# RWKV attention, FFN and top-1 MoE chained on one core: the first three attention tiles re-queued over VectorE and GpSimd, and the raw-weight transposes moved behind the third product

## The chip, the cores and the metric

The kernel runs on one core of one Trainium2 chip. The metric is device time of one launch in microseconds (us), and a kernel's time is the median of its runs.

## What is computed

Three stages follow one another, each on 3072 tokens (4 batches of 768) of 384 features (8 heads of 48), in fp32 with fp64 inputs for the weights of the last two:

```python
# 1. attention, per batch and head
for t in range(S):
    cur = einsum('bhd,bhe->bhde', u * k[t], v[t])
    y[t] = einsum('bhd,bhde->bhe', r[t], state + cur)
    state = w * state + einsum('bhd,bhe->bhde', k[t], v[t])
# 2. FFN, 384 -> 2048 -> 384
h = x @ w_in
g = h - tanh(h)
x = g @ w_out
# 3. top-1 mixture, 8 experts of 384 -> 1024 -> 384
xn, en = x / |x|, emb / |emb|
logits = xn @ en.T / tau
out = gate * (relu(x @ w1[e]) @ w2[e])   # e = argmax(logits)
```

## The kernel before

**Attention** works on 24 tiles of 128 tokens, three to a block of 384 tokens. With the decay tables `tab_r` and `tab_k` (powers of w along the tile, built by `decay_tables`, lines 194 to 208) a tile is a few matrix products. `Att` holds its steps: `products` multiplies r by k (L376), `decay_r` and `decay_k` scale r and k by the tables (L355, L358), `summed` sums the products per head with u (TensorE L382, copied by ScalarE L384), `diagonal` writes those sums on a diagonal (ScalarE L405, eight instructions, tile `am`), `scores` multiplies keys by queries (L423, PSUM tiles `pa`), `causal` copies the lower triangle of the scores over `am` (VectorE L428, two instructions), `values` multiplies by the values (L454, PSUM tile `py`), and `result_hi` and `result_lo` write the result as a rounded part and the rest (ScalarE L459, VectorE L462). `turned` and `turned_rows` transpose the scaled keys (L364) and copy them out (ScalarE L369, `ktok`); `state_product` (L475) and `state_add` carry the state on.

**The FFN** goes over its 2048 hidden features in steps of 128. `ffn1` computes one step for a block: nine matmuls of 128x384 (L557), since activations and weights are both split in a rounded and a rest part. `squares` and `small_tanh` turn its result into h - tanh(h) (from ScalarE L612 on), and `ffn2` multiplies that by w_out into three accumulators (L572). The weights come as fp64 chunks; `convert` turns the bits into fp32 on VectorE (L264, L267, L270, each in two pieces), and `split` makes the two parts on ScalarE (L277) and GpSimd (L278). The first chunk is converted and split in two halves, the others whole. The odd chunks hold w_out; `Logits.turn` transposes such a raw chunk (six TensorE transposes L293, two copies L295) for products with the expert embeddings (L303).

**PSUM** has eight banks, handed out in the order in which the program asks. A filler is a matmul on a tile of ones whose result is overwritten (`fill`, L547): `scores`, `values` and `ffn1` take their number as `idle`, and the table `IDLE` gives it for the first six steps of the main loop.

**Order.** Each engine works through its queue in program order, and the opening (lines 1310 to 1386) is written out by hand: the steps of tiles `a[0]` to `a[2]`, the first chunk's conversion, and the expert embeddings' norms (`embedding_norms` ScalarE L1243, `embedding_roots` VectorE L1246 and a GpSimd power L1247, `embedding_rows` VectorE L1250 to L1252). Then the first two products of the first block (`early`) are issued, and the loop over `steps` (L1442 on) issues one product for each step, with a piece of the following tiles (`attention_stage`: the fourth to sixth tile), a chunk's conversion and, where due, `Logits.turn`, `done` and `load_next`, which starts the next chunk's load. The third product is that of step 2, the fourth that of step 3. The first accumulation of `ffn2` stands behind the fifth product, and from there on the products and accumulations of the FFN follow one another.

## Time and profile before

| what | value |
|---|---|
| median of 3 runs | 769.78 us |
| lowest and highest run | 769.21 us, 770.74 us |
| profiled execution, its own time | 771.22 us |
| its span, first to last instruction | 769.6 us |
| mean granted clock of TensorE in it | 0.995 |
| TensorE busy | 756.2 us, 98% of the span |

The profiled execution lies 1.44 us above the median, and 1.6 us of its time lie outside the span. Times inside it are microseconds from the start of the span. TensorE's work is busy time as the profiler's records model it, so a busy share says that something was in the array, not that it ran at full clock; the granted clock is a column of its own.

### The profile page before, as it was taken

The numbers are of one execution on the slowest core, as the hardware profiler recorded it, in microseconds if no ns is written. First come the engines' busy times: TensorE is split into PE (matmuls) and PEld (weight loads), VectorE is DVE, ScalarE is ACT, GpSimd is POOL, SyncE is SP. The second block draws the span as 40 slices with busy tenths as digits, with TensorE's granted clock in tenths as the row PEclk, the third lists the DMA queues.
The fourth block names the chain that finished last, engine by engine and source line by source line (L and its number), as shares of the span: only waits on it lengthen the run. The fifth ranks groups of instructions, "written<-read, shape, count | busy, mean of one in ns | idle before, by whom it ended". The sixth has DMA issues, their size and how long they took to land.

```text
span 769.6 us, 15995 instructions
## 1 busy us (share of the span) xinstructions
PE 756.2 (98%) x6143; PEld 718.4 (93%) x6143; DVE 464.8 (60%) x1037; ACT 457.1 (59%) x1064; POOL 300.5 (39%) x362
## 2 busy tenths in 40 slices
PE   9899999999999999999999999999999999999996
PEld 5689899999999999999999999999989999999996
DVE  7967976667656565565555655656684455545430
ACT  5787676655657556656657756768463535544431
POOL 3743680466781671753564341133530202110111
PEclk9899999999999999999999999999999999999999
DMA  8964355243240330232223101052374435454400
GB/s 263 288 206 142 118 170 200 64 165 100 66 148 24 126 122 2 91 94 87 80 69 123 59 32 64 14 171 85 116 229 143 129 115 189 150 173 161 154 31 32
DMA packets 41016, 92.21 MB, mean 120 GB/s; under 512 B 4827, under 2 KB 20597, under 8 KB 39907
## 3 DMA queue, kind: packets, MB, share of 16 engines
q1 hardware_dynamic: 36274, 81.44, 33.0%
q0 software_dynamic: 4240, 9.67, 3.5%
q8 instruction: 50, 0.82, 0.4%
q14 instruction: 36, 0.29, 0.1%
q10 hardware_dynamic: 416, 0.00, 0.0%
HBM read 67.26 MB, written 24.00 MB: 119 GB/s over the span
## 4 chain that ended last, share of the span: by engine, by line
PE 90%; issue 3%; DVE 3%; ACT 2%; DMA 2%; POOL 1%; POOLq 0%; SPq 0%; DVEq 0%; ACTq 0%
PE acc L572 39%; PE ph L557 37%; PE py L454 5%; PE pa L423 3%; DMA eraw<-in_moe_w_dram 2%; PE pt L908 1%; PE warm L158 1%; PE pst L475 1%; POOL out_dram L827 0%; PE pt L293 0%; DVE bits L267 0%; DVE wraw L270 0%; PE pl L303 0%; DVE bits L264 0%; PE accn L1036 0%
## 5 line engine op out<-in xcount | busy, mean ns | idle before, releaser
L557 PE MATMUL ph<-xt,wq 128*128 128x384 f32 (+4 forms) x1712 | 340.1, 341 | 1.9 <-ACT wt L295 1.3
L557 PEld LDWEIGHTS ph<-xt,wq 128*128 128x128 f32 x1712 | 302.7, 188 | 5.9 <-ACT wt L295 1.5
L572 PE MATMUL acc<-wq,ghi 128*128 128x392 f32 (+2 forms) x1120 | 289.1, 343 | 0.9 <-ACT ghi L625 0.9
L572 PEld LDWEIGHTS acc<-wq,ghi 128*128 128x128 f32 (+1 forms) x1120 | 200.3, 187 | 5.9 <-ACT ghi L625 1.2
L572 PE MATMUL acc<-wq,glo 128*128 128x392 f32 (+2 forms) x552 | 182.2, 340 | 0.1
L612 ACT ACTIVATE z<-ph 128x384 f32<-128x384 f32 x128 | 62.8, 490 | 105.0 <-PE ph L557 104.7
L623 DVE TENSOR_TENSOR ph<-ph,z 128x384 f32<-128x384 f32 x128 | 72.0, 563 | 62.6 <-ACT z L612 62.0
L572 PEld LDWEIGHTS acc<-wq,glo 128*128 128x128 f32 (+1 forms) x552 | 102.7, 187 | 0.9 <-DVE glo L635 0.7
L635 DVE TENSOR_TENSOR glo<-ph,ghi 128x384 fp32r<-128x384 f32 x128 | 70.7, 553 | 45.7 <-ACT ghi L625 45.6
L827 POOL DMA_INDIRECT out_dram<-ob,gts x27 | 27.2, 1008 | 176.6 <-ACT ob L917 171.4
L625 ACT ACTIVATE ghi<-ph 128x384 fp32r<-128x384 f32 x128 | 62.6, 490 | 41.0 <-DVE ph L624 37.6
L615 ACT ACTIVATE q<-z,sb_t 128x384 f32<-128x384 f32 x128 | 78.9, 617 | 3.4
L624 DVE SCALAR_TENSOR_TENSOR ph<-q,ph 128x384 f32<-128x384 f32 x128 | 71.7, 560 | 12.5 <-ACT q L615 3.5
L629 ACT ACTIVATE mk<-z,lz_t 128x384 bf16<-128x384 f32 x128 | 77.1, 603 | 0.0
L653 DVE SCALAR_TENSOR_TENSOR glo<-ph,ghi 128x384 fp32r<-128x384 f32 (+2 forms) x56 | 30.7, 549 | 63.8 <-ACT ghi L651 63.8
L651 ACT ACTIVATE ghi<-ph 128x384 fp32r<-128x384 f32 (+4 forms) x56 | 27.5, 491 | 67.6 <-PE ph L557 67.5
L411 POOL TENSOR_TENSOR am<-ident,cd 128x512 f32<-128x512 f32 x36 | 36.8, 1045 | 77.8 <-DVE cd L397 77.1
L886 DVE TENSOR_TENSOR wq<-eraw,wq 128x768 fp32r<-128x768 f32 x60 | 55.1, 955 | 11.5 <-ACT wq L885 11.0
L885 ACT ACTIVATE wq<-eraw 128x768 fp32r<-128x768 f32 x64 | 50.4, 839 | 6.2 <-DMA eraw<-in_moe_w_dram 6.2
L278 POOL TENSOR_TENSOR wq<-wraw,wq 128x768 fp32r<-128x768 f32 (+1 forms) x17 | 30.3, 1782 | 39.6 <-ACT wq L277 38.5
L716 POOL DMA_INDIRECT tab<-tk,irow x24 | 24.4, 1019 | 31.8 <-DVE tk L744 25.1
L491 POOL TENSOR_TENSOR st<-st,pw 112x384 f32<-112x384 f32 x20 | 16.7, 840 | 49.2 <-DVE st L484 43.7
(287 smaller groups left out, 860.0 us busy)
## 6 DMA issues: line engine op xcount, KB each, us to landing
eraw<-in_moe_w_dram SPq DMA_DIRECT2D x32, 768.0 KB, 4.5
rkv<-in_rows_dram SPq DMA_DIRECT2D x18, 640.0 KB, 5.6
tt<-in_cols_dram SPq DMA_DIRECT2D x22, 448.0 KB, 4.4
xd<-xt SPq DMA_DIRECT2D x8, 1152.0 KB, 8.0
wraw<-in_moe_w_in_dram SPq DMA_DIRECT2D x8, 768.0 KB, 8.6
wraw<-in_moe_w_out_dram SPq DMA_DIRECT2D x8, 768.0 KB, 5.2
rkv<-xe SPq DMA_DIRECT2D x22, 192.0 KB, 4.4
xe<-zero SPq DMA_DIRECT2D x2, 1536.0 KB, 15.4
```

The costliest lines, as they stand in the source:

```text
L454: nc.tensor.matmul(out=self.py[32 * g:32 * g + 32, kk, :], lhsT=lhs, rhs=rhs, start=start, stop=stop)
L557: mark["ph"] = nc.tensor.matmul(out=ph, lhsT=lhs[a][:, kk, :], rhs=rhs(b, kk), start=(kk == 0 and p == 0), stop=(kk == nk - 1 and p == 2)).ins
L572: mm = nc.tensor.matmul(out=acc[t][:lhs.shape[1]], lhsT=lhs, rhs=rhs(b, i), start=(i == span[0] and p == 0), stop=(i == span[1] - 1 and p ...
L612: nc.scalar.activation(out=z, in_=ph, func=AF.Square)
L615: nc.scalar.activation(out=q, in_=z, func=AF.Square, scale=SS, bias=sb_t)
L623: nc.vector.tensor_tensor(out=ph, in0=ph, in1=z, op=ALU.mult)
L624: nc.vector.scalar_tensor_tensor(out=ph, in0=q, scalar=KC, in1=ph, op0=ALU.add, op1=ALU.mult)
L625: mark["ghi"] = nc.scalar.activation(out=ghi, in_=ph, func=AF.Copy).ins
L629: nc.scalar.activation(out=mk, in_=z, func=AF.Relu, bias=lz_t, accum_out=zx[:, step:step + 1])
L635: mark["glo"] = nc.vector.tensor_tensor(out=glo, in0=ph, in1=ghi.bitcast(F32), op=ALU.subtract).ins
L885: nc.scalar.activation(out=hi[c][:, a], in_=t[:, a], func=AF.Copy)
L886: engs[s % len(engs)].tensor_tensor(out=lo[c][:, a], in0=t[:, a], in1=hi[c][:, a].bitcast(F32), op=ALU.subtract)
```

## The change

The diff leaves the number of matmuls of the computation as it is. It moves these things in the opening:

- The products of `a[0]` and `a[1]` go from VectorE to GpSimd, behind `routing_constants`. `a[2].decay_k` and the fourth tile's `decay_r` (`a[TB]`) also go to GpSimd.
- The third tile's `products`, decays and `summed` come ahead of the first `values`, and `diagonal` of the third tile ahead of its `scores`.
- Fillers: `a[0].scores` 4 to 1, `a[0].values` 2 to 0, `a[2].scores` 2 to 0, `a[1].values` 3 to 0, `a[2].values` 5 to 2, and 6 to 0 ahead of the third product.
- The second half of the first chunk is converted behind the low parts of all three tiles, and the norms of the embeddings come behind the third tile's result, their power behind the fourth tile's products on GpSimd.
- The first `Logits.turn`, with `done(1)` and `load_next()`, goes from the end of step 1, ahead of the third product, to right behind that product.

```diff
@@ -87,7 +87,7 @@
     LIST = {0: (), 2: (4, 10), NB - 1: (), NB: (10,)}
     FA = 6
     START = (0, 1, 2)
-    IDLE = (0, 0, 6, 4, 4, 3)
+    IDLE = (0, 0, 0, 4, 4, 3)
     CONV = (0, 1, 2, 3, 5, 6, 7, 8, 9, 11, 12, 13, 15, 18)
     nxt = None
     nars = {}
@@ -191,7 +191,7 @@
         nc.vector.memset(half[:, TB:], 1e-9)
         nc.vector.memset(ent, 0.0)
 
-    def decay_tables(between):
+    def decay_tables():
         def square(i):
             nc.vector.tensor_tensor(out=pw[:, :, i + 1:i + 2], in0=pw[:, :, i:i + 1], in1=pw[:, :, i:i + 1],
                                     op=ALU.mult)
@@ -201,8 +201,6 @@
         nc.vector.reciprocal(out=tab_r[:, :, 0:1], in_=w64)
         for i in range(7):
             n = 1 << i
-            if i == 5:
-                between()
             nc.vector.tensor_tensor(out=tab_r[:, :, n:2 * n], in0=tab_r[:, :, 0:n],
                                     in1=pw[:, :, i:i + 1].to_broadcast([PW, HP, n]), op=ALU.mult)
         nc.scalar.activation(out=tab_k, in_=tab_r[:, :, ::-1], func=AF.Copy)
@@ -1310,67 +1308,65 @@
     nc.sync.dma_start(out=u_bc, in_=u.rearrange("(o h) d -> o h d", o=1).to_broadcast([P, H, D]))
 
     a = [Att(n, xts[0]) for n in range(TB)]
-    decay_tables(lambda: a[0].products(nc.vector))
+    routing_constants()
+    decay_tables()
+    for t in a[:2]:
+        t.products(nc.gpsimd)
+    for x in st:
+        nc.gpsimd.memset(x, 0.0)
     a[0].summed()
-    a[0].decay_r(nc.vector)
-    a[0].decay_k(nc.vector)
-    a[0].scores(range(HP), 4)
+    for t in a[:2]:
+        t.decay_r(nc.vector)
+        t.decay_k(nc.vector)
+    a[0].scores(range(HP), 1)
     a[0].turned()
     a[0].diagonal(True)
-    routing_constants()
-    for x in st:
-        nc.gpsimd.memset(x, 0.0)
-    a[1].products(nc.vector)
-    a[1].decay_r(nc.vector)
-    a[1].decay_k(nc.vector)
     a[1].summed()
     a[1].scores(range(HP))
     a[1].turned()
     a[1].diagonal(True)
-    small_constants()
-    embedding_norms()
     a[0].causal()
-    a[0].values(idle=2)
-    a[0].result_hi()
     a[2].products(nc.vector)
     a[2].decay_r(nc.vector)
-    a[2].decay_k(nc.vector)
+    a[2].decay_k(nc.gpsimd)
     a[2].summed()
-    a[2].scores(range(HP), 2)
+    small_constants()
     a[1].causal()
-    embedding_roots()
-    a[0].result_lo()
+    a[0].values()
     a[2].diagonal(True)
-    a[1].values(idle=3)
+    a[2].scores(range(HP))
+    a[0].result_hi()
+    a[1].values()
     a[1].result_hi()
     ops = convert_next()
     for _ in range(2):
         next(ops)
     a[2].causal()
+    a[0].result_lo()
     next(ops)
     split(*ready[0], i=0)
+    a[2].values(idle=2)
+    a[1].result_lo()
+    a[2].result_hi()
+    a[2].result_lo()
+    embedding_norms()
     a.append(Att(TB, None))
     a[TB].products(nc.gpsimd)
-    a[2].values(idle=5)
-    a[1].result_lo()
-    a[2].result_hi()
-    for _ in range(2):
-        next(ops)
-    a[2].result_lo()
     for _ in ops:
         pass
+    embedding_roots()
     last = split(*ready[0], i=1)
     done.add(0)
     a[0].turned_rows()
     a[1].turned_rows()
     load_next()
     a[TB].decay_k(nc.gpsimd)
+    a[TB].decay_r(nc.gpsimd)
     embedding_rows()
     early = [ffn1([win(p, 0) for p in range(2)], columns_of(xts[0]), NK, TOK, by_part=True)]
     a[0].state_product()
     early.append(squares(early[0], a[0].state_add))
     convert_now(True)
-    a[TB].decay_r(nc.vector)
     mark["pool"] = split(*ready[2])[1]
     done.add(2)
     early.append(ffn1([win(p, 1) for p in range(2)], columns_of(xts[0]), NK, TOK))
@@ -1451,6 +1447,10 @@
             xt = xts[j]
             ph = ffn1([win(p, f) for p in range(2)], columns_of(xt), NK, TOK, IDLE[i] if i < len(IDLE) else 0) \
                 if i > 1 else early[2 * i]
+            if i == 2:
+                logits[0].turn()
+                done.add(1)
+                load_next()
             if 0 in accs and spill:
                 part = stage(0, [P, TB, DL], F32, "part")
                 for t, x in enumerate(accs.pop(0)):
@@ -1488,8 +1488,9 @@
         if i in turns:
             c = turns[i]
             logits.append(Logits(c, ready[2 * c + 1][0]))
-            logits[c].turn()
-            done.add(2 * c + 1)
+            if c:
+                logits[c].turn()
+                done.add(2 * c + 1)
         if m < NF:
             last = split(*ready[m])
             if m % 2 == 0:
```

The line numbers of the changed kernel are two lower from the middle of the file on (L557 becomes L555). Three places of the queues, with what an instruction waits for in brackets (an engine's signal, or a DMA queue's).

TensorE ahead of the fourth product, before (`pl` is the logits' product, `pt` the transposes of the second raw chunk, `ph<-ones_94` the first of four fillers):

```order
L303 MATMUL pl<-wt,ent 32x128 x5
L293 MATMUL pt<-ident,wraw 128x128 [waits DMAHW1_49,Activation_49]
L293 MATMUL pt<-ident,wraw 128x128 x2
L293 MATMUL pt<-ident,wraw 128x128 [waits DVE_49]
L547 LDWEIGHTS ones_94
L547 MATMUL ph<-ones_94 128x384 [waits DVE_49]
```

and in the changed kernel:

```order
L301 MATMUL pl<-wt,ent 32x128 x5
L291 MATMUL pt<-ident,wraw 128x128 [waits DMAHW1_49,Activation_49]
L291 MATMUL pt<-ident,wraw 128x128 x2
L291 MATMUL pt<-ident,wraw 128x128 [waits DVE_49]
L545 LDWEIGHTS ones_94
L545 MATMUL ph<-ones_94 128x384 [waits Activation_49]
```

The instructions are the same. The banks are handed out in a new order, so that the first filler waits for ScalarE and no longer for VectorE. Followed through the banks and the signals counted, that is ScalarE's copy of the fifth tile's turned keys (`ktok`), and the second half of the transposes waits for the first `causal` instruction of the fifth tile.

ScalarE between the two chunk splits (`wq_78<-wraw`), before:

```order
L295 ACTIVATE wt<-pt 128x384 [waits PE_49]
L277 ACTIVATE wq_78<-wraw 128x2x384 [waits DMAHW6_49,DVE_49]
L295 ACTIVATE wt<-pt 128x384 [waits PE_49]
L277 ACTIVATE wq_78<-wraw 128x2x384 [waits DMAHW1_49,DVE_49]
L612 ACTIVATE z<-ph 128x384 [waits PE_49]
L486 ACTIVATE st_127<-pst 48x4x48 [waits PE_49,Pool_49]
```

and in the changed kernel:

```order
L275 ACTIVATE wq_78<-wraw 128x2x384 [waits DMAHW6_49,DVE_49]
L293 ACTIVATE wt<-pt 128x384 [waits PE_49] x2
L627 ACTIVATE mk,zx<-z,lz_t 128x384 [waits Activation_49]
L610 ACTIVATE z<-ph 128x384
L484 ACTIVATE st_127<-pst 48x4x48 [waits PE_49,Pool_49]
L613 ACTIVATE q<-z,sb_t 128x384 [waits Activation_49]
L627 ACTIVATE mk,zx<-z,lz_t 128x384
L382 ACTIVATE cd<-ps_cd 128x8 [waits PE_49]
L275 ACTIVATE wq_78<-wraw 128x2x384 [waits DMAHW1_49,DVE_49]
```

The second of the two splits goes behind the third product's first steps (L610 on). Last, VectorE around the embeddings' norms, before:

```order
L267 SCALAR_TENSOR_TENSOR bits<-wraw,bits 128x384 [waits DVE_49]
L462 TENSOR_TENSOR xt<-py,xt 128x3x128 [waits Activation_49]
L270 SCALAR_TENSOR_TENSOR wraw<-wraw,bits 128x3x128 [waits DVE_49]
L1250 RECIPROCAL rtau<-tau_t 128x1 [waits DMAHW3_49]
L1251 TENSOR_SCALAR en_n<-en_n 8x1 [waits Pool_49]
L1252 RECIPROCAL en_n<-en_n 8x1 [waits DVE_49]
L264 TENSOR_SCALAR bits<-wraw 128x512 [waits DMAHW5_49]
```

and in the changed kernel:

```order
L460 TENSOR_TENSOR xt<-py,xt 128x3x128 [waits Activation_49] x2
L262 TENSOR_SCALAR bits<-wraw 128x384 [waits DVE_49]
L265 SCALAR_TENSOR_TENSOR bits<-wraw,bits 128x384 [waits DVE_49]
L268 SCALAR_TENSOR_TENSOR wraw<-wraw,bits 128x3x128 [waits DVE_49]
L1244 TENSOR_SCALAR en_n<-en_n 8x1 [waits Activation_49]
L1248 RECIPROCAL rtau<-tau_t 128x1 [waits DMAHW3_49]
L1249 TENSOR_SCALAR en_n<-en_n 8x1 [waits Pool_49]
L1250 RECIPROCAL en_n<-en_n 8x1 [waits DVE_49]
L262 TENSOR_SCALAR bits<-wraw 128x512 [waits DMAHW5_49]
```

The half chunk's three steps (`bits`, 128x384) now all stand behind the third tile's low part, and the maximum L1244, whose power on GpSimd L1249 waits for, stands three rows ahead of the next chunk's conversion. On GpSimd that power stands directly behind the fourth tile's products.

## Rows read from the trace of the kernel before

**Rows 1.** The page: span, busy time of each engine.

```profile
span 769.6 us, 15995 instructions
...
PE 756.2 (98%) x6143; PEld 718.4 (93%) x6143; DVE 464.8 (60%) x1037; ACT 457.1 (59%) x1064; POOL 300.5 (39%) x362
```

**Rows 2.** Timeline of TensorE: start, us, engine, line, operation, count, idle before.

```profile
29.13 0.60 PE L364 MATMUL ps_k<-ident,tt 112*128 112x112 f32 x4
31.57 1.13 PE L293 MATMUL pt<-ident,wraw 128*128 128x128 f32 x4 [1.84 <-DVE wraw L270]
...
34.06 2.12 PE L547 MATMUL ph<-ones 128*128 128x384 bf16 x6
35.73 2.79 PE L557 MATMUL ph<-xt,wq 128*128 128x384 f32 x9
...
42.39 1.17 PE L293 MATMUL pt<-ident,wraw 128*128 128x128 f32 x6
43.58 0.81 PE L547 MATMUL ph<-ones 128*128 128x384 bf16 x4
44.09 1.89 PE L557 MATMUL ph<-xt,wq 128*128 128x384 f32 x9
```

**Rows 3.** Windows: us, busy of PE, PEld, DVE, ACT, POOL, clock, DMA share.

```profile
25.45:44.45 19.00, 16.28 (x142) 13.05 (x141) 17.33 (x36) 16.40 (x45) 11.01 (x7) 0.82 0.76 238
28.00:30.00 2.00, 1.73 (x18) 1.40 (x17) 2.00 (x6) 1.61 (x5) 1.55 (x2) 1.00 1.01 296
30.00:32.00 2.00, 0.43 (x2) 0.43 (x3) 2.00 (x5) 2.00 (x8) 1.89 (x2) 0.72 1.05 392
35.71:37.70 1.99, 1.99 (x8) 1.99 (x7) 1.95 (x5) 0.01 (x1) 1.56 (x1) 0.50 0.60 147
29.73:38.45 8.72, 6.02 (x23) 4.43 (x22) 7.93 (x15) 6.69 (x18) 6.07 (x4) 0.61 0.90 306
```

**Rows 4.** Timeline of ScalarE, same stretch.

```profile
25.45 0.93 ACT L277 ACTIVATE wq<-wraw 128x768 fp32r<-128x768 f32 x1
...
37.70 0.90 ACT L277 ACTIVATE wq<-wraw 128x768 fp32r<-128x768 f32 x1 [1.99 <-DVE wraw L270]
...
43.98 0.47 ACT L369 ACTIVATE ktok<-ps_k 128x384 f32<-128x384 f32 x1
```

**Rows 5.** Timeline of VectorE: norms, the conversion behind them, later steps.

```profile
21.33 0.56 DVE L462 TENSOR_TENSOR xt<-py,xt 128x384 fp32r<-128x384 f32 x1
21.81 0.55 DVE L270 SCALAR_TENSOR_TENSOR wraw<-wraw,bits 128x384 int32<-128x384 int32 x1
...
22.34 0.12 DVE L1251 TENSOR_SCALAR en_n<-en_n 8x1 f32<-8x1 f32 x1
...
24.41 1.00 DVE L270 SCALAR_TENSOR_TENSOR wraw<-wraw,bits 128x512 int32<-128x512 int32 x2
...
31.77 1.40 DVE L355 TENSOR_TENSOR tt<-tt,tab_r 112x512 f32<-112x512 f32 x1
...
42.80 0.73 DVE L428 COPY_PREDICATED am<-cmask,pa 128x512 f32<-128x512 uint8 x1
```

**Rows 6.** Timeline of GpSimd: the power, the fourth tile's products, a decay.

```profile
15.75 0.58 POOL L1247 TENSOR_TENSOR en_n<-en_n,half 8x1 f32<-8x1 f32 x1 [8.99 <-DVE en_n L1246]
...
21.85 1.30 POOL L376 TENSOR_TENSOR rows<-tt 112x512 f32<-112x512 f32 x1 [0.47 <-DMA tt<-in_cols_dram]
...
32.57 1.74 POOL L358 TENSOR_TENSOR cols<-cols,tab_k 112x512 f32<-112x512 f32 x1
```

**Rows 7.** Timeline of VectorE in the opening.

```profile
6.48 0.68 DVE L376 TENSOR_TENSOR rows<-tt 112x512 f32<-112x512 f32 x1
7.08 0.74 DVE L206 TENSOR_TENSOR tab_r<-tab_r,pw 112x128 f32<-112x128 f32 x2
```

**Rows 8.** Timeline of TensorE in the opening.

```profile
4.69 3.25 PE L158 MATMUL warm<-ones 128*128 128x512 bf16 x9
...
21.35 1.91 PE L557 MATMUL ph<-xt,wq 128*128 128x384 f32 x9 [0.61 <-ACT xt L459]
```

## The prediction, made before the changed kernel had run

> **What bounds the kernel now.** I read the page first. TensorE is busy for 756.2 of 769.6 us [rows 1], so a gain must come from stretches in which it stands idle, does work that counts for nothing, or runs at half clock. The timeline of TensorE shows where: between the fourth tile's turned keys (L364, over at 29.13 + 0.60 = 29.73) and the third tile's state product at 38.45 it does six transposes of raw weights and the third product, and around them the rows show 1.84 us of idle time, six fillers, and a product of 2.79 us where the fourth product takes 1.89 [rows 2]. The windows say why that product is long: granted clock 1.00 from 28 to 30 us, when TensorE was busy for 1.73 of 2 us, 0.72 in the two after, with 0.43 busy, and 0.50 from 35.71 on [rows 3]. Those are the two levels, 2.4 and 1.2 GHz. Behind the fourth product, at 44.09, TensorE has its accumulations and hardly waits again, so I follow the start of that product: what it gains or loses is what the kernel gains or loses.
>
> The same windows show the other engines in that stretch. From the split of the second converted chunk (L277 at 25.45) to the copy of the fifth tile's turned keys (L369, over at 43.98 + 0.47 = 44.45) ScalarE is busy for 16.40 of 19.00 us, and 1.99 of its 2.60 idle us are one hole ahead of its next-but-one split, waiting for a conversion on VectorE [rows 3, 4]. VectorE is busy for 17.33 of 19.00 [rows 3]. So two helpers are nearly as full as TensorE here.
>
> **The change, step by step.** *Third product and transposes.* They need 1.89 and 1.17 us at full clock [rows 2], 3.06 together, where 8.72 us passed [rows 3]. If nothing else bound, 8.72 - 3.06 = 5.66 us would go. The fillers taken out there are part of it.
>
> *What is late next.* The fillers ahead of the fourth product used to wait for VectorE: its L428 at 42.80 lasts 0.73 and ends at 43.53, and the first filler starts at 43.58 [rows 2, 5]. In the changed order they wait for ScalarE's copy of the fifth tile's keys. Between the first filler and the product lie 44.09 - 43.58 = 0.51 us [rows 2]. So the fourth product now starts no sooner than that copy's end plus about 0.5.
>
> *ScalarE's stretch.* Between its two ends it holds the same instructions as before, with the later split moved behind the third product's first steps. That fills the hole of 1.99, whose conversion is then no longer waited for. The other 0.61 us of idle time may stay or go: the stretch shrinks by 1.99 to 2.60 us, no more.
>
> *Where the stretch starts.* It starts with the split of a chunk whose conversion on VectorE follows the norms' additions (L1251). From the start of L1251 at 22.34 to the end of the conversion at 24.41 + 1.00 = 25.41 are 3.07 us [rows 5]. L1251 waits for a power on GpSimd, which was long done at 15.75 + 0.58 [rows 6]. Now the power stands behind the fourth tile's products, and these wait for that tile's columns from DRAM: they start at 21.85 and take 1.30 [rows 6]. So the power ends no sooner than 21.85 + 1.30 + 0.58 = 23.73, the conversion at 26.80, 1.4 us later than before. The other way to the power is through VectorE: the third tile's low part ends at 21.33 + 0.56 = 21.89, and now three conversion steps of about 0.55 stand behind it [rows 5], then the maximum, which I take at 0.12 as L1251's row, then the power and the conversion: 21.89 + 1.65 + 0.12 + 0.58 + 3.07 = 27.31, 1.9 later, less what the opening gains. I take 1.5 us.
>
> *Sum.* Keys' copy done at 44.45 + 1.5 - 1.99 = 43.96 with the small gaps kept, 43.35 with all closed; plus 0.51, the fourth product starts at 44.47 or 43.86, against 44.09. With 1.4 or 1.9 in place of 1.5 the ends are 43.76 and 44.87. That is -0.3 to +0.8 us, and I take **+0.2**. The 5.66 us are nearly all given back, because ScalarE's queue is not shorter and starts later.
>
> *VectorE.* Its conversion at the end of the hole shifts by +1.5, but a decay of the fourth tile leaves its queue (0.68, the duration of an operation of that size [rows 7]), and one that took 1.40 [rows 5] may take 0.68 again. It costs nothing as long as the split that reads it stands behind the third product's first steps; without that cover it would cost up to the 1.99 us again.
>
> *The opening.* Two products of 0.68 [rows 7] leave VectorE for GpSimd, where one takes 1.30 [rows 6]. The first lies beside the warm-up matmuls, which last until 4.69 + 3.25 = 7.94 [rows 8]. Some fillers go too, each about 0.2 (0.81 for four [rows 2]), five of them directly ahead of values. The first product, at 21.35 [rows 8], may come 0 to 0.7 us sooner. That buys nothing further on than the floor of 1.4 above, since the fourth tile's columns set it.
>
> *Beside each other.* Products on GpSimd run beside VectorE's table multiplications (L206, two in 0.74 [rows 7]) and its first decays. The trace shows what such a meeting costs: a decay on VectorE took 1.40 beside one on GpSimd, twice 0.68, and the next on GpSimd 1.74 in place of 1.30 [rows 5, 6, 7]. One meeting on the path costs 0 to 0.72, and I take it as using up the opening's gain. The Trainium skill, "SBUF — State Buffer", section "Who interferes with whom", says more: the two engines share a port pair under an exclusive lock, and a VectorE operation with two SBUF inputs waits until a GpSimd operation that reads SBUF is over. By that rule a meeting would be estimated at up to 1.3 us instead of 0.72, and the sum would rise by up to 0.6.
>
> **Rivals.** *The clock falls later (slower).* The changed kernel has no fillers around the third product, and its TensorE waits twice where before it worked: the third tile's state product waits for the fourth tile's `causal`, and half the second transposes wait for the fifth tile's. Before, the clock fell after 2 us with 0.43 busy [rows 3]. If two such gaps put it to half ahead of the fourth product, that takes 2.79 instead of 1.89, and its four fillers 4 x 2.12/6 = 1.41 instead of 0.81 [rows 2]: 0.90 + 0.60 = 1.5. It decides once TensorE is let run at 0.50 when the fourth product starts. With +0.2 that is +1.7. For it: the idle gaps move closer to the fourth product. Against it: the third product now runs at full clock and fills 3 us. Chance 0.32.
>
> *ScalarE does not bind (faster).* If the keys' copy is not what the fillers wait for, or it comes early, the 5.66 us less the later start of 1.5 remain: -4.2 us, 765.6. For it speaks that TensorE's idle and half-clock time is real; against it, the 16.40 busy us in ScalarE's stretch, which no part of the change takes away. Chance 0.12.
>
> *The opening comes later.* Two meetings on the path, 1.44 us, add to VectorE's way to the power: 27.31 + 1.44 = 28.75, 3.3 later in place of 1.5, hence +0.2 + 1.8 = +2.0, 771.8. Against it: TensorE has its warm-up beside the first. Chance 0.08.
>
> **How the numbers follow.** The sum is made in the profiled execution: 771.22 + 0.2 = 771.4 us. The median of the runs lies 1.44 below that execution, and I forecast against it: 769.78 + 0.2 = **770.0 us**. My forecast (ScalarE decides, clock full) has 0.48. Differences below 0.2%, 1.5 us, count as none, since a measurement of this kernel can hardly tell them. Forecast all same: 0.48. Clock: its +1.7 lies at the border, so 0.21 slower and 0.11 same. Opening: 0.08, 0.07 slower. Faster is the second rival, 0.12. So faster 0.12, same 0.60, slower 0.28. The range reaches from 768.3 (the sum's lower end of -0.3, and 1.2 us of the 1.53 between the lowest and the highest run) to 771.8 (the clock's and the opening's prices) and leaves out the faster rival and a tail above, under 0.2 together.
>
> **What would show it.** Right: the fourth product starts at 44.1 +/- 0.8; the third starts near 31 instead of 35.73 and takes 1.9; the split that opens ScalarE's stretch starts near 27, and the hole of 1.99 is gone; the fillers ahead of the fourth product wait for `ktok` of ScalarE. Clock rival: a granted clock near 0.5 between 40 and 47 us and a fourth product of 2.8. Opening rival: a split that starts after 28. The forecast is wrong if the fourth product starts before 43, or if TensorE loses or gains over 1 us anywhere behind it.

## The result, and the profile after

The changed kernel takes 776.07 us (median of 6 runs, 774.46 to 777.06) where the kernel before took 769.5 in the same comparison (768.72 to 771.77). The ratio is 1.0078, with a 95% interval of 1.006 to 1.0095: some 6 us **slower**, outside the range that was given. The profiled execution took 776.13 us, its span is 774.5 us, and its mean granted clock is 0.985, where it was 0.995.

TensorE's timeline shows how much was lost by when (columns as in [rows 2]; line numbers are two lower):

```profile
8.73 0.32 PE L545 MATMUL pa<-ones 128*128 128x384 bf16 x1
9.81 1.90 PE L421 MATMUL pa<-tt 48*128 48x128 f32 x16 [0.76 <-DVE tt L356]
...
12.45 1.73 PE L380 MATMUL ps_cd<-u_pair,rows 112*128 112x2 f32 x8
...
18.58 1.93 PE L452 MATMUL py<-am,rkv 128*32 128x128 f32 x32
...
26.16 1.92 PE L555 MATMUL ph<-xt,wq 128*128 128x384 f32 x9 [0.61 <-ACT xt L457]
29.36 0.56 PE L473 MATMUL pst<-rkv,ktok 128*48 128x48 f32 x16 [1.28 <-ACT ktok L367]
29.86 1.86 PE L555 MATMUL ph<-xt,wq 128*128 128x384 f32 x9
...
36.56 1.86 PE L555 MATMUL ph<-xt,wq 128*128 128x384 f32 x9 [0.62 <-DVE wraw L268]
38.25 0.87 PE L291 MATMUL pt<-ident,wraw 128*128 128x128 f32 x6
40.75 0.56 PE L473 MATMUL pst<-first,ktok 128*48 128x48 f32 x16 [1.62 <-DVE am L426]
...
48.24 1.44 PE L545 MATMUL ph<-ones 128*128 128x384 bf16 x4 [0.23 <-ACT ktok L367]
49.23 2.69 PE L555 MATMUL ph<-xt,wq 128*128 128x384 f32 x9
```

The first product (L555, the first row of that line) starts at 26.16, where it started at 21.35 [rows 8]: **4.81 us are lost before it**. The third starts at 36.56 and takes 1.86, at full clock, as forecast; it was at 35.73 with 2.79 [rows 2]. The fourth starts at 49.23, which is 23.07 behind the first; before it was 44.09 - 21.35 = 22.74. The first accumulation follows at 59.37 instead of 53.46, 5.9 later, and of this about 1 us is won back further on (the spans differ by 4.9).

The windows of the changed kernel show why (columns as in [rows 3]):

```profile
8.00:10.00 2.00, 1.24 (x11) 0.99 (x13) 1.74 (x4) 1.50 (x5) 0.57 (x1) 1.00 1.09 254
12.00:22.00 10.00, 10.00 (x86) 9.24 (x86) 5.33 (x14) 4.21 (x15) 2.04 (x2) 0.50 1.04 344
32.22:48.20 15.98, 13.44 (x112) 11.35 (x113) 15.98 (x34) 15.86 (x45) 11.72 (x8) 0.87 0.55 171
38.00:41.00 3.00, 1.38 (x20) 1.22 (x20) 3.00 (x6) 3.00 (x9) 2.80 (x3) 1.00 0.95 296
44.00:50.00 6.00, 5.67 (x30) 3.67 (x30) 5.03 (x11) 5.88 (x18) 2.65 (x2) 0.51 0.51 147
```

From 8 to 10 us TensorE was busy for 1.24 of 2 us; it had one filler and then waited for VectorE's decays until 9.81. From then on the clock is at its lower level: 0.50 from 12 to 22 us, ten microseconds in which TensorE is busy throughout, so that everything there takes nearly twice as long. The sums of a tile (L380) take 1.73 at 12.45, and the second tile's scores 2.08 at 14.11. In the kernel before, at full clock, the same sums and the first scores are

```profile
9.33 1.16 PE L423 MATMUL pa<-tt 48*128 48x128 f32 x16
...
10.86 0.96 PE L382 MATMUL ps_cd<-u_pair,rows 112*128 112x2 f32 x8
```

A second lull, 1.38 of 3 us busy from 38 to 41 us, is followed by 0.51 from 44 to 50, and there the fourth product takes 2.69 instead of 1.89 [rows 2]. The window from 32.22 to 48.20 shows ScalarE's stretch: 15.86 of 15.98 us busy, where it was 16.40 of 19.00 [rows 3].

VectorE's timeline, for the steps of the sum [rows 5, 7]:

```profile
5.58 2.80 DVE L204 TENSOR_TENSOR tab_r<-tab_r,pw 112x4 f32<-112x4 f32 x7
...
10.93 0.69 DVE L353 TENSOR_TENSOR tt<-tt,tab_r 112x512 f32<-112x512 f32 x1 [1.17 <-POOL rows L374]
...
26.14 0.56 DVE L460 TENSOR_TENSOR xt<-py,xt 128x384 fp32r<-128x384 f32 x1 [0.80 <-ACT xt L457]
...
29.10 0.14 DVE L1249 TENSOR_SCALAR en_n<-en_n 8x1 f32<-8x1 f32 x1 [0.62 <-POOL en_n L1245]
...
31.19 1.00 DVE L268 SCALAR_TENSOR_TENSOR wraw<-wraw,bits 128x512 int32<-128x512 int32 x2
```

Seven table multiplications now take 2.80 us beside GpSimd's first product; before, five took 1.07 and the last two 0.74 (the latter in [rows 7]):

```profile
5.50 1.07 DVE L206 TENSOR_TENSOR tab_r<-tab_r,pw 112x4 f32<-112x4 f32 x5
```

The second tile's decay (10.93) waits 1.17 us for GpSimd's second product, because it overwrites what that product reads. The last three rows are the chain that was forecast: the third tile's low part, the norms' addition waiting for GpSimd's power, and the conversion, over at 32.19.

ScalarE's stretch begins and ends with (as in [rows 4])

```profile
32.22 0.91 ACT L275 ACTIVATE wq<-wraw 128x768 fp32r<-128x768 f32 x1 [0.88 <-DVE wraw L268]
...
47.73 0.46 ACT L367 ACTIVATE ktok<-ps_k 128x384 f32<-128x384 f32 x1
```

and the fillers ahead of the fourth product start at 48.24, released by that copy of the keys, as the TensorE rows above say.

### The profile page after: what moved, and what is told of

It reads as the page before. It is cut to its first block, busy times and chain, and to the rows that moved or that the text cites. A ratio compares the mean times of both kernels' runs of the same rounds, so it can differ in the third digit from the quotient of the medians.

```text
span 774.5 us, 15960 instructions
## 1 busy us (share of the span) xinstructions
PE 760.0 (98%) x6124; PEld 723.5 (93%) x6124; DVE 463.5 (60%) x1033; ACT 456.8 (59%) x1064; POOL 307.1 (40%) x366
## 4 chain that ended last, share of the span: by engine, by line
PE 88%; issue 3%; ACT 3%; DVE 2%; DMA 2%; POOL 1%; SPq 0%; POOLq 0%; DVEq 0%
PE acc L570 38%; PE ph L555 37%; PE py L452 5%; PE pa L421 3%; DMA eraw<-in_moe_w_dram 1%; PE pt L906 1%; PE pst L473 1%; ACT am L403 1%; POOL out_dram L825 0%; PE pt L291 0%; PE pl L301 0%; PE ps_cd L380 0%; ACT wq L275 0%; PE accn L1034 0%; PE ph L1034 0%
## 5 line engine op out<-in xcount | busy, mean ns | idle before, releaser
L555 PE MATMUL ph<-xt,wq 128*128 128x384 f32 (+4 forms) x1712 | 340.0, 341 | 2.6 <-ACT wt L293 1.3
L555 PEld LDWEIGHTS ph<-xt,wq 128*128 128x128 f32 x1712 | 302.5, 188 | 6.7 <-ACT wt L293 1.5
L610 ACT ACTIVATE z<-ph 128x384 f32<-128x384 f32 x128 | 62.7, 490 | 110.4 <-PE ph L555 110.2
```

Of the source, the lines that this page charges most:

```text
L555: mark["ph"] = nc.tensor.matmul(out=ph, lhsT=lhs[a][:, kk, :], rhs=rhs(b, kk), start=(kk == 0 and p == 0), stop=(kk == nk - 1 and p == 2)).ins
L610: nc.scalar.activation(out=z, in_=ph, func=AF.Square)
```

## The experiments

Two theories to begin with. **Clock:** the opening leaves TensorE too little to do, the clock falls there, and this is the loss. **Chain:** the new order and GpSimd's products delay the values whatever the clock. Each kernel ran beside the kernel before on one chip, but not all on the same one, so kernels of different comparisons are set beside each other by their ratios. This table holds what their traces say: the mean granted clock in two windows, the starts of the first product, the fourth product and the first accumulation, the time of that profiled execution, and the ratio of the medians with its interval.

| kernel | clock 8 to 26 | clock 26 to 54 | 1st product | 4th | 1st acc | its time | ratio to before |
|---|---|---|---|---|---|---|---|
| before | 1.00 | 0.88 | 21.35 | 44.09 | 53.46 | 771.22 | |
| changed | 0.62 | 0.88 | 26.16 | 49.23 | 59.37 | 776.13 | 1.0078 (1.006 to 1.0095) |
| e1 changed, first filler back | 0.62 | 0.88 | 27.16 | 50.22 | 60.27 | 777.07 | 1.0084 (1.0055 to 1.0114) |
| e2 changed, all fillers back | 0.72 | 0.88 | 27.05 | 51.24 | 60.98 | 778.53 | 1.0083 (1.0052 to 1.0115) |
| e3 changed, products on VectorE | 0.72 | 0.88 | 23.98 | 47.71 | 57.53 | 775.86 | 1.0051 (1.0034 to 1.0069) |
| e4 before, first filler cut | 0.81 | 0.94 | 24.37 | 46.11 | 55.61 | 771.75 | 1.0004 (0.9989 to 1.002) |
| e5 before, later transposes | 1.00 | 0.82 | 21.22 | 42.95 | 52.33 | 768.25 | 1.0002 (0.9987 to 1.0017) |
| e6 changed, transposes back | 0.72 | 0.94 | 24.64 | 46.48 | 56.23 | 774.77 | 1.007 (1.0045 to 1.0096) |
| e7 changed, many fillers | 1.00 | 0.82 | 23.34 | 45.86 | 55.47 | 771.37 | 1.0049 (1.0024 to 1.0074) |
| e8 before, products on GpSimd | 0.91 | 0.88 | 23.35 | 45.73 | 55.08 | 771.76 | 1.001 (0.9994 to 1.0026) |
| e9 changed, norms back | 0.62 | 0.77 | 27.12 | 53.35 | 63.39 | 780.22 | 1.0068 (1.0044 to 1.0091) |
| e10 before, third tile's order | 1.00 | 0.88 | 23.07 | 45.67 | 55.05 | 772.27 | 1.002 (1.001 to 1.0031) |
| e11 before, late norms | 1.00 | 0.88 | 21.23 | 44.98 | 54.39 | 771.34 | 1.0019 (1.0011 to 1.0028) |
| e12 e7 and e9 together | 1.00 | 0.70 | 23.38 | 47.67 | 57.59 | 774.89 | 1.0056 (1.0042 to 1.0071) |
| e13 e12, transposes back | 1.00 | 0.88 | 23.31 | 45.99 | 55.69 | 771.9 | 1.0042 (1.0027 to 1.0056) |
| e14 e5 with fillers | 1.00 | 0.82 | 21.28 | 45.95 | 56.12 | 773.0 | 1.0029 (1.0018 to 1.004) |
| e15 before, all fillers cut | 0.62 | 0.88 | 25.78 | 47.92 | 57.47 | 774.86 | 0.9991 (0.9976 to 1.0005) |
| e16 e7, third tile's old order | 1.00 | 0.82 | 23.49 | 47.62 | 56.94 | 774.1 | 1.0041 (1.0025 to 1.0057) |
| e17 before again | 1.00 | 0.88 | 21.20 | 44.41 | 53.76 | 770.99 | 1.0001 (0.9987 to 1.0014) |

In all nineteen the last matmul ends 708.3 to 710.8 us behind the first accumulation, so the column "1st acc" decides the time of a profiled execution to within 2.5 us. In the second window no kernel, the one before included, has a clock of 1.00: each profile has a fall somewhere between 26 and 54 us.

### Fillers and products in the changed kernel: e1, e2, e3

e1 puts the first tile's four fillers back, e2 all of them, e3 puts the products back on VectorE.

```diff
 e1  a[0].scores(range(HP), 1) -> 4
 e2  a[0].scores 4, a[0].values 2, a[2].scores 2, a[1].values 3, a[2].values 5
 e3  decay_tables(lambda: a[0].products(nc.vector)); a[1].products(nc.vector)
```

> The changed kernel with only the first tile's scores filler back from 1 to 4. Clock theory: in the changed kernel TensorE had 1.24 of 2 us busy from 8 to 10 us and ran at clock 0.50 from 12 to 22, which put the first product at 26.16 instead of 21.35; with the fillers back TensorE is busy until the scores, the clock stays at 1.00, the first product starts at 21 to 22, and the time falls by 4 to 5 us, to 771 to 772. Chain theory (products on GpSimd and the third tile's earlier steps delay the values, whatever the clock): the clock may rise, but the first product stays at 25 or later and the time within 1.5 us of the changed kernel's 776.

> The changed kernel with all opening fillers of the kernel before (4, 2, 2, 3, 5). Clock theory: as with the four fillers alone, first product at 21 to 22.5, 771 to 772; the later fillers cost at most 0.5 us of the first product's start. Chain theory: first product at 25 or later, 776 to 777.

> The changed kernel with the first two tiles' products back on VectorE, few fillers as in the change. Chain theory: the values come sooner, first product at 21 to 22, time 771 to 772. Clock theory: with one filler ahead of the first scores TensorE is still light from 8 to 12 us, the clock falls to 0.50 there and the time stays at 774 to 777.

The clock theory's forecasts failed for e1 and e2: 776.74 and 777.3 us in the median, no better than the change. But the clock had not come back either (0.62 and 0.72), so they do not speak against the clock, only against the old number of fillers as a cure. In e1 the first scores came later still, at 10.82. Its VectorE and GpSimd rows show what they waited for:

```profile
9.00 1.76 DVE L356 TENSOR_TENSOR tt<-tt,tab_k 112x512 f32<-112x512 f32 x1
```

```profile
8.55 1.66 POOL L374 TENSOR_TENSOR rows<-tt 112x512 f32<-112x512 f32 x1 [1.11 <-DMA tt<-in_cols_dram]
```

A decay that takes 0.69 alone ran from 9.00 to 10.76; GpSimd's product ran from 8.55 to 10.21. In the profile of the change the same product came only at 9.43, when its columns had landed; the decay had begun at 9.07 and took 0.69. So the lateness of the first scores differs between executions.

e3 was at 774.92 us with its first product at 23.98, the clock at 0.72: half clock stays, and most of the loss with it, as the clock theory says. The first product is 2.2 us sooner than in the profile of the change, where the chain theory gave 21 to 22. But e6 below, whose opening is that of the change line by line, has it at

```profile
24.64 1.91 PE L555 MATMUL ph<-xt,wq 128*128 128x384 f32 x9 [0.76 <-ACT xt L457]
```

so the opening of the change costs 4.81 us in one execution and 3.29 in another, and the 2.2 us can't be put down to GpSimd's products. The intervals of e3 and of the change overlap too, so the size of their share stays open.

### Parts of the change alone: e4, e5, e8, e10, e11, e15

Each is the kernel before with one part of the change.

```diff
 e4   a[0].scores(range(HP), 4) -> 1
 e15  e4, and a[0].values, a[2].scores, a[1].values 0, a[2].values 2
 e5   IDLE[2] 6 -> 0; logits[0].turn() behind the third product
 e8   a[0], a[1].products(nc.gpsimd) behind routing_constants()
 e10  a[2].products, decays, summed ahead of a[0].values; a[2].diagonal ahead of a[2].scores
 e11  embedding_norms(), embedding_roots(), second half of chunk 0 behind a[2].result_lo()
```

> The kernel before with only the first tile's scores filler cut from 4 to 1. Clock theory: the clock falls to 0.50 at 10 to 12 us as in the changed kernel, first product 2 to 5 us later, time 772 to 775. Chain theory: nothing on the path changes, within 0.7 us of the kernel before.

> The kernel before with one part of the change alone: the first raw-weight transposes behind the third product, and no fillers ahead of it. ScalarE theory (the fourth product waits for the copy of the fifth tile's keys): the split that opens ScalarE's stretch starts where it did, the stretch shrinks from 19.0 to about 16, and the fourth product starts 1 to 2.5 us sooner against the first product than the 22.7 us before, so 0.5 to 2.5 us faster than before. Clock theory: TensorE idles twice around the third tile's state product, the clock falls to 0.50 ahead of the fourth product, which takes 2.3 to 2.8 us, and 0.8 to 1.5 us are given back: within 1 us of the kernel before.

> The kernel before with one part of the change alone: the products of the first two tiles on GpSimd. Contention theory: VectorE's table multiplications, seven of which took 2.80 us in the changed kernel beside GpSimd's first product, take 1 us longer than before, a decay may take 1.7 instead of 0.7 beside the second, the first scores start 0.5 to 1.7 us later, and with the clock falling in that wait the first product comes 2 to 5 us later: 771 to 774. If the products are harmless and only the order and the fillers count: within 0.7 us of the kernel before.

> The kernel before with one part of the change alone: the third tile's products, decays and sums ahead of the first values, with the fillers as before. Order theory: the first values move behind 0.7 us of sums and VectorE's three steps, TensorE waits there, the clock falls, and the first product comes 1 to 4 us later: 771 to 774. If the order is harmless by itself: the same within 0.8 us of the kernel before, first product at 20.7 to 22.5.

> The kernel before with one part of the change alone: the embeddings' norms and the first chunk's second half behind the third tile's result. Norms theory: second product 3.5 to 3.9 us behind the first instead of 2.52, split 1.5 to 2 us later, fourth product 1 to 2 us later: 771 to 772. If ScalarE's stretch absorbs it: the same within 0.8 us of the kernel before.

> The kernel before with all its opening fillers cut as in the change (1, 0, 0, 0, 2), and nothing else. If the missing fillers by themselves let the clock fall in the opening for as long as in the changed kernel (12 to 14 us at 0.50): first product at 24 to 26, time 772 to 774. If the clock falls for no longer than with the first filler cut alone (6.8 us) or the delay is absorbed: within 1 us of the kernel before.

**Clearly slower alone** are the third tile's order (771.75 us, ratio 1.002) and the late norms (771.77, 1.0019). e11 shows the norms' price as it was worked out ahead:

```profile
21.23 1.91 PE L557 MATMUL ph<-xt,wq 128*128 128x384 f32 x9 [0.61 <-ACT xt L459]
24.42 0.56 PE L475 MATMUL pst<-rkv,ktok 128*48 128x48 f32 x16 [1.29 <-ACT ktok L369]
24.92 1.85 PE L557 MATMUL ph<-xt,wq 128*128 128x384 f32 x9
```

The first product stands where it stood, the second comes 3.69 behind it instead of 23.87 - 21.35 = 2.52, and the keys' copy releases the state product 1.29 us late. The price behind it is 0.5 to 1 us at the fourth product: 23.75 behind the first, where the two profiles of the kernel before have 22.74 and 23.21 (e17 below). In e10 the clock is full through the opening and the first product still comes at 23.07, because ScalarE writes the third tile's diagonals from 15.57 on, ahead of the first result at 17.92 (14.93 before), and VectorE's queue behind it waits (2.85 us for that result); the order costs 1.7 us there without the clock, which its expectation had put down to a fall.

**Not told from before** are the products on GpSimd (770.68; in the profile the first scores start later, at 9.76, the clock falls for a short time, and the first product comes at 23.35), the later transposes (770.57) and the fillers (770.34 for one place, 770.07 for all). In e4, one place, the profile had the fall that the clock theory gave, with the first product at 24.37, and the median did not move. The expectation for e15 failed in its median and was met in its profile: twelve executions took 769.13 to 774.86 us, and the profiled one, the longest, has

```profile
8.16 0.32 PE L547 MATMUL pa<-ones 128*128 128x384 bf16 x1
9.29 1.16 PE L423 MATMUL pa<-tt 48*128 48x128 f32 x16 [0.81 <-DVE tt L358]
...
12.12 2.08 PE L423 MATMUL pa<-tt 48*128 48x128 f32 x16
...
15.06 1.94 PE L454 MATMUL py<-am,rkv 128*32 128x128 f32 x32
...
25.78 1.91 PE L557 MATMUL ph<-xt,wq 128*128 128x384 f32 x9 [0.62 <-ACT xt L459]
```

TensorE idle for 0.81 us ahead of the first scores, until VectorE's decay is done, then values in 1.94 where they take 1.08, and the first product at 25.78, as late as in the change. So one and the same program lies up to 5.7 us apart from execution to execution; that the others held the clock is inferred from their times, as only one has a profile.

e5 tests the forecast's central sum by itself, and its ScalarE theory held in the profile:

```profile
30.85 3.25 PE L557 MATMUL ph<-xt,wq 128*128 128x384 f32 x9 [1.21 <-DVE glo L635]
...
42.95 1.94 PE L557 MATMUL ph<-xt,wq 128*128 128x384 f32 x9
```

The fourth product starts 21.73 behind the first, 1 to 1.5 us sooner than in the two profiles of before, although the third took 3.25 at half clock. In the median nothing is left of it.

### Holding the clock: e7, e16, e6, e9, e12, e13, e14

```diff
 e7   a[0].scores 12, a[1].scores 4, a[0].values 3, a[2].scores 3, a[1].values 3, a[2].values 5
 e16  e7, a[2].products to summed, diagonal and scores behind a[0].values again
 e6   IDLE[2] 0 -> 6; logits[0].turn() at the end of step 1 again
 e9   embedding_norms(), embedding_roots(), second half of chunk 0 ahead of a[2].result_lo()
 e12  e7 and e9        e13  e7, e9 and e6
 e14  e5, a[3].scores(range(HP), 4), a[4].scores(range(HP), 3)
```

> The changed kernel with many fillers in the opening (12, 4, 3, 3, 3, 5), enough to bridge TensorE's idle time ahead of the first and second scores. Clock theory: the granted clock stays at 1.00 from 8 to 25 us, the values then run at full speed and the first product starts at 21.5 to 23.5, which gives 771 to 773. Chain theory (third tile's work ahead of the first values, GpSimd's products): the clock stays up and the first product still starts at 25 or later, 775 or more.

> The changed kernel with the opening's fillers (12, 4, 3, 3, 3, 5) and the third tile's steps back behind the first values, where they stood before. Order theory: with the clock held, the first product of the filled kernel still came at 23.34, because the third tile's diagonal waits for the first values to free its buffer and its scores for TensorE; in the old order it comes at 21.5 to 22.3, and the time falls by 1 to 1.5 us from 772.8, to 771 to 772. Rival (the first product is late because of GpSimd's products and the twelve fillers ahead of the first scores, which start at 10.4 instead of 9.3): first product at 22.8 or later, time within 0.7 us of 772.8.

> The changed kernel with the transposes and the six fillers back ahead of the third product: the opening's part of the change alone. If the opening is the whole loss, the time is 775 to 777 and the fourth product comes 25 us or more behind the first, since its start shifts with the norms. If the later transposes are the loss (half clock at the fourth product), it falls to 770 to 773.

> The changed kernel with the embeddings' norms and the first chunk's second half back where they stood (ahead of the third tile's low part), everything else as changed. Norms theory: in the changed kernel the second product came 3.70 us behind the first instead of 2.52, and the chunk split that opens ScalarE's stretch 6.06 us behind it instead of 4.10; these go back to 2.5 and about 4.2, the fourth product comes 21 to 22 us behind the first instead of 23.07, and the time falls by 1 to 2 us, to 774 to 775. Clock theory alone: the first product and half clock stay, and the norms cost nothing behind it: 775.5 to 777.

> The changed kernel with both repairs, the many fillers of the opening (12, 4, 3, 3, 3, 5) and the norms back in place. If half clock in the opening and the late norms are together the loss: first product at 23.3, second at 25.9, fourth at 44 to 45.5, time 770 to 772, within 1.5 us of the kernel before. If a third cause is at work: still 773 or more.

> The changed kernel with three repairs: the opening's fillers (12, 4, 3, 3, 3, 5), the norms back in place, and the transposes with their six fillers back ahead of the third product. What stays of the change are the products and decays on GpSimd and the third tile's order. Clock theory: the 17 us at clock 0.50 between the third and fourth products of the same kernel with the later transposes shrink to 7 or less, the first accumulation comes at 54.5 to 55.5 instead of 57.59, and the time falls from 774.8 to 771 to 772.5. Rival (the transposes' place does not matter once ScalarE's stretch decides): 774 to 775.5.

> The kernel before with the transposes behind the third product, and 4 and 3 fillers ahead of the fourth and fifth tiles' scores to hold the clock there. Clock theory: the two stretches at 0.50 behind 29 us shrink or go, the fourth product starts at 41.5 to 43 instead of 44.09, and the time falls to 767 to 769.5. Rival: the fillers delay the scores and keys by up to 1.4 us, ScalarE's stretch with them, and the time is the same or up to 1 us longer than before, 770 to 771.5.

e7 tests the clock in the opening. Its rows:

```profile
8.36 2.11 PE L545 MATMUL pa<-ones 128*128 128x384 bf16 x12
10.39 1.16 PE L421 MATMUL pa<-tt 48*128 48x128 f32 x16
...
11.93 0.97 PE L380 MATMUL ps_cd<-u_pair,rows 112*128 112x2 f32 x8
...
23.34 1.92 PE L555 MATMUL ph<-xt,wq 128*128 128x384 f32 x9 [0.61 <-ACT xt L457]
...
33.72 3.25 PE L555 MATMUL ph<-xt,wq 128*128 128x384 f32 x9 [0.47 <-DVE wraw L268]
...
45.86 2.17 PE L555 MATMUL ph<-xt,wq 128*128 128x384 f32 x9
```

Twelve fillers bridge the wait for the decays, the clock is 1.00 from 8 to 26, the second tile's sums take 0.97 where the change took 1.73, and the first product starts at 23.34 instead of 26.16: 2.8 us sooner, although the fillers themselves push the first scores from 9.81 to 10.39. That is the clock theory's forecast, and the chain theory's (25 or later) is out.

One profile could be luck, and e7's is the fastest of its six executions; but e12, e13 and e16 below have the same fillers, and all four profiles have the clock at 1.00 and the first product at 23.31 to 23.49, where the five changed kernels with GpSimd's products and no more fillers than before (the change, e1, e2, e6, e9) have 0.62 to 0.72 and 24.64 to 27.16.

The median falls from 776.07 to 772.84 us, which the intervals of the two ratios (1.0078 and 1.0049) don't tell apart; those of e13 and e16 lie clear of the change's, with other edits besides. Which of the six places of fillers holds the clock was not tried.

In e7's profile 2 us of lateness stay against 21.35. e16 asked whether the third tile's order makes them, and the answer is no here: with the old order (the first result's low part stays late) the first product comes at 23.49, and its ratio of 1.0041 is not told from e7's. What stays is the first scores' start, 10.39 and 10.47 against 9.33, and the added fillers: from there to the first product are 12.95 us in e7 and 12.02 before.

The other five show that a lull moved from one place opens another. e6 (transposes back) is 1 us faster than the change, within the intervals; its fourth product runs at full clock, 21.84 behind the first and not the 25 or more that its expectation gave. e9 was to win the norms' 1 to 2 us and won nothing: 777.41 us in the median, with executions from 770.66 to 780.22. In its profile, the longest, the clock fell between the third and the fourth product, and these lie 16.6 us apart. e12 shows the same with a held opening: at 774.81 us it missed the 770 to 772 of its expectation, whose other branch, a third cause, is what came. e13 shows what it takes to mend it:

```profile
32.56 3.25 PE L555 MATMUL ph<-xt,wq 128*128 128x384 f32 x9 [0.81 <-DVE wraw L268]
...
47.67 2.47 PE L555 MATMUL ph<-xt,wq 128*128 128x384 f32 x9
```

```profile
36.27 2.96 PE L555 MATMUL ph<-xt,wq 128*128 128x384 f32 x9
...
45.99 1.89 PE L555 MATMUL ph<-xt,wq 128*128 128x384 f32 x9
```

In e12 the fourth product lies 15.1 us behind the third, in e13 9.7, and its first accumulation comes 1.9 sooner, at 55.69 where 54.5 to 55.5 was expected. The expectation of 771 to 772.5 for e13 was met by its profiled execution (771.9) and missed by its median (773.88), whose interval overlaps e12's.

e14 was the attempt to beat both kernels. Its fillers held the clock through the third product, and then it fell:

```profile
30.90 1.86 PE L557 MATMUL ph<-xt,wq 128*128 128x384 f32 x9 [0.57 <-DVE glo L635]
...
35.15 0.56 PE L475 MATMUL pst<-first,ktok 128*48 128x48 f32 x16 [1.63 <-DVE am L428]
...
45.95 2.72 PE L557 MATMUL ph<-xt,wq 128*128 128x384 f32 x9
```

The third product takes 1.86, the state product then waits 1.63 us for VectorE, and the fourth comes at 45.95 at half clock, 3 us later than without the fillers. 773.14 us: worse than before, and outside both branches of its expectation. No version of these beats the kernel before.

### The kernel before once more: e17

> The kernel before once more, unchanged, for a second profile. If its opening holds the clock as a rule: clock 1.00 from 8 to 29 us, first product at 21.2 to 21.4, ratio 1.000 within 0.1%. If the first profile was a lucky one: half clock before 20 us, first product at 23 or later.

```profile
9.17 1.16 PE L423 MATMUL pa<-tt 48*128 48x128 f32 x16 [0.33 <-DVE tt L358]
...
21.20 1.91 PE L557 MATMUL ph<-xt,wq 128*128 128x384 f32 x9 [0.61 <-ACT xt L459]
...
44.41 1.88 PE L557 MATMUL ph<-xt,wq 128*128 128x384 f32 x9
```

It held the clock in its opening a second time. All the profiles with the first two tiles' steps and fillers of before (before, e5, e10, e11, e14, e17) did: TensorE was idle for 0 to 0.33 us ahead of the first scores. So did the four with many fillers. In those in which it fell (the change, e1, e2, e3, e4, e6, e8, e9, e15) it was idle there for 0.53 to 1.88 us. This sorts the profiles and is not a rule: in e10 TensorE is idle for longer ahead of the third values,

```profile
20.77 0.41 PE L454 MATMUL py<-am,first 128*32 128x128 f32 x4 [1.24 <-issue]
```

and the clock stays at 1.00 up to 32 us.

The fourth product of e17 lies 44.41 - 21.20 = 23.21 behind the first, where the first profile had 22.74. So differences of half a microsecond between two profiles at that place say nothing.

## Why the prediction was wrong

**The step that failed is the opening's**: "The first product, at 21.35 [rows 8], may come 0 to 0.7 us sooner." It came 4.81 us later. I counted what left VectorE's queue and the time that fillers take, and not what the fillers were for: with one filler in place of four, and with decays that come later, TensorE waits ahead of the first scores, the clock goes to half, and for ten microseconds it is busy throughout at 0.50. e7 holds the clock with more fillers and gives 2.8 of the 4.81 back, although those fillers take time too. I had the mechanism as a rival, but put it ahead of the fourth product only, at 1.5 us, with its price from one product and four fillers.

**The clock rival at its own place came true**: the fourth product took 2.69, its fillers 1.44 us instead of 0.81. Starts of the fifth product follow: 8.42 behind the fourth instead of 7.65, so 0.8 us.

**The central sum held, counted from the first product, but in part by luck.** It said -0.3 to +0.8 with +0.2 taken for the fourth product; measured is 23.07 - 22.74 = +0.33, and -0.14 against the 23.21 of e17. Its terms: the conversion was to end at 27.31 by VectorE's way, with the opening as before; it ended at 32.19, and 32.19 - 4.81 = 27.38. The split of ScalarE moved with it, by 32.22 - 25.45 - 4.81 = 1.96 more than the opening: the upper of the two ways, where I took 1.5. ScalarE's stretch shrank by 19.00 - 15.98 = 3.02, more than the 2.60 of idle time, since it was also busy for 0.5 us less. The first filler ahead of the fourth product waited for the keys' copy, as read from the order, but from that copy's end to the product were 49.23 - 48.19 = 1.04 us, where I took 0.51 from fillers at full clock. So I had the start 0.46 too low, the gap 0.53 too low and the shrinkage 0.4 to 1.0 too low, and these errors cancel for the most part. What e11 and e5 do alone fits in sign: the late norms cost 0.5 to 1 us at the fourth product, the later transposes win 1 to 1.5 us there.

**Beside each other.** Two meetings were priced at 0 to 0.72 us each, from the row of 1.40 [rows 5]. The first cost 2.80 - 1.07 - 0.74 = 1.0 us, on the path to the first scores. In e1 the decay took 1.76 instead of 0.69, 1.07 more. Each was above 0.72 and below 1.3. That is the side of the Trainium skill, "SBUF — State Buffer", section "Who interferes with whom": a VectorE operation with two SBUF inputs contends with a GpSimd operation that reads SBUF, under an exclusive lock, and the order of issue decides which of the two waits. In e1 GpSimd's product started first (8.55 against 9.00) and the decay ended 0.55 us behind it, nearly the 0.69 of a whole decay; in the change the decay started first (9.07 against 9.43) and took 0.69. Both traces agree with it. What I missed besides is a plain dependence: `decay_r` overwrites in place what GpSimd's product reads, so a slower product (1.47 instead of 0.68) holds VectorE's queue for 1.17 us.

**The third tile's order** I costed at nothing. Alone it takes 1.6 us (e10). In the filled kernel its removal gained nothing (e16), so its share in the 6 us is not settled. Nor is that of the interplay: the parts alone sum to -0.8 (fillers, e15) + 0.6 (e8) + 1.6 (e10) + 1.6 (e11) + 0.5 (e5) = 3.5 us by their medians, of which only the order and the norms are told from nothing by their intervals, and the whole is 6. The traces of the change point to half clock in the opening for the rest, but no run isolates it; why the clock falls in all six timed executions of the change (mean 0.981 to 0.988 in each) and only in some of e15's is not shown.

**The chances.** Slower by over 0.2% had 0.28. The range ended at 771.8 since each rival was priced alone; the opening and the clock were the same event.

## What to carry to other kernels

Fillers and short waits on TensorE are priced by what happens to the clock behind them, not by their own time: before one is cut, or a wait is put ahead of small matmuls, take the TensorE work that follows at twice its duration for the upper end of the range. A lull that is mended in one place can open where the work is thin next (e9, e12, e14), so a version is judged by several executions, not by one profile. And when an operation moves to a slower engine, look for who overwrites its inputs: the wait turns up on the engine that was relieved.

## What the runs showed of the hardware

- From 12 to 22 us of the change TensorE was busy for all of 10 us with small matmuls, and the clock was 0.50 throughout; with fillers put between the same matmuls (e7) it was 1.00 there. A busy share alone does not tell the clock.
- A VectorE multiplication of 112x512 beside a GpSimd one of the same size took 1.76 us in place of 0.69 (e1), and table multiplications of 1.81 us took 2.80.
- Executions of one program lay 9.6 us apart (e9: 770.66 to 780.22), where those of the kernel before lay 4.4 apart in the same comparison (768.48 to 772.89).
